# Loading the first six tiles as two halves of 64 partitions on two DMA queues

## The chip, the cores and the metric

The kernel runs on one core of a Trainium2 chip. The metric is the device time of one execution in microseconds (us); lower is better.

## The reference

A channel gate. The input is 384 x 384 pixels of 384 channels in bf16, 113 MB. The mean of each channel goes through a one-tap filter and a sigmoid, and scales that channel everywhere.

```python
g = jnp.einsum("bhwc->bc", x) / (H * W)
s = sigmoid(g * w1d[0])
return x * s[:, None, None, :]
```

## The kernel before

All of x is read once and all of the output is written once. 147,456 pixels are 1152 rows on each of 128 partitions; they are cut into 26 tiles of 45 or 44 rows (8 of 45, 18 of 44). The on-chip ring has room for six tiles.

Loads are issued by SP (SyncE), stores by ACT (ScalarE). Each of the two has its own DMA queue (q1 and q10 on the page of the kernel before, 3744 and 3746 packets). The profile counts 16 DMA engines, and in the packet records about 16 rows are in flight at a time, whether they come from one queue or from two; so the same 16 engines are taken to serve both. In the profile's lines PE is TensorE and DVE is VectorE. TensorE adds up every tile with a matrix of ones. After three tiles a provisional sigmoid `s_early` is taken from the rows seen so far, and VectorE multiplies tiles by it and ACT stores them. At the end the true sigmoid is compared with `s_early` bit for bit; only if they differ would a second pass run (in no run shown here did it). So the time is one pass over the data.

```python
TILE = 45
AHEAD_TILES = 3
...
plan.dma("scalar", w_one[0:1, 0:1], w1d.unsqueeze(0), writes=["w_one"])   # weight first
... # warm up the sigmoid's table; matmul and scaling of the weight

def load(place, n, r0):
    plan.dma("sync", at(place, n), dram(x_rows, r0, n), writes=rows(place, n))
...
for k, n in enumerate(sizes):
    place = ring.take(n)
    while inside and any(p < place + n and place < p + m for p, m, _ in inside):
        put(*inside.pop(0))          # multiply by s_early (vector), store (scalar queue)
    load(place, n, r0)
    inside.append((place, n, r0))
    add_rows(...)                    # n matmuls with ones
    if k == AHEAD_TILES - 1:
        ... # total <- acc (vector); s_early <- sigmoid(total) (scalar)
```

`plan` writes one instruction stream per engine in program order and puts semaphore waits where data need them. A load of a 45-row tile writes 34,560 bytes to each of 128 partitions, and in the trace it is 128 packets of that size. Below, "a row" of a load means such a packet of one partition.

Of the kernel before, what the change touches and what calls it, by code (L numbers as in the profile page):

```python
# [3 lines left out]
P = 128  # L4
# [5 lines left out]
ACT_F = mybir.ActivationFunctionType  # L10
# [113 lines left out]
TILE = 45  # L124
# [3 lines left out]
def bass_standalone__channel_attn_eca__vision_kernel(  # L128
# [7 lines left out]
    n_rows = B * H * W // P  # L136
    x_rows, o_rows = x.flatten_outer_dims(), out.flatten_outer_dims()

    def dram(view, r0, n):
        return view[r0 * P : (r0 + n) * P, :].rearrange("(p t) c -> p (t c)", p=P)  # L140

    ones = nc.alloc_sbuf_tensor("ones", [P, P], BF16)
    s_early = nc.alloc_sbuf_tensor("s_early", [P, C], BF16)
    s_true = nc.alloc_sbuf_tensor("s_true", [P, C], BF16)
    w_one = nc.alloc_sbuf_tensor("w_one", [1, 16], BF16)
    w_scaled = nc.alloc_sbuf_tensor("w_scaled", [P, 2], F32)
    warm = nc.alloc_sbuf_tensor("warm", [P, 2], F32)
# [3 lines left out]
    n_arena = nc.sbuf_bytes_remaining // (2 * C)  # L151
    arena = nc.alloc_sbuf_tensor("arena", [P, n_arena * C], BF16)
    acc = [nc.alloc_psum_tensor(f"acc{i}", [P, 512], F32) for i in range(3)]

    def at(r0, n):
        assert r0 + n <= n_arena
        return arena[:, r0 * C : (r0 + n) * C]

    def rows(r0, n):
        return [("sb", r) for r in range(r0, r0 + n)]  # L160

    def gate(place, n, s):
        s_b = s[:].unsqueeze(1).broadcast_to([P, n, C])
# [4 lines left out]
    early_rows = sum(sizes[:AHEAD_TILES])  # L168
    plan = Planner(nc, "a", 50)


    plan.op("gpsimd", lambda e: e.memset(warm[:, 0:1], 0.0), writes=["warm"])  # L172
    plan.op("vector", lambda e: e.memset(ones[:], 1.0), writes=["ones"])  # L173
    plan.dma("scalar", w_one[0:1, 0:1], w1d.unsqueeze(0), writes=["w_one"])
    plan.op(
        "scalar",
        lambda e: e.activation(warm[:, 1:2], warm[:, 0:1], ACT_F.Sigmoid),  # L177
        reads=["warm"],
        writes=["warm1"],
    )  # L180
    plan.op(
        "tensor",
        lambda e: e.matmul(  # L183
            acc[2][:, 0:1], ones[0:1, :], w_one[0:1, 0:1], start=True, stop=True
        ),
        reads=["ones", "w_one"],
        writes=["acc2"],
    )
    for i, n in enumerate((early_rows, n_rows)):
        plan.op(  # L190
            "vector",
            lambda e, i=i, n=n: e.tensor_scalar_mul(  # L192
                w_scaled[:, i : i + 1], acc[2][:, 0:1], 1.0 / float(P * n)
            ),
            reads=["acc2"],
            writes=[f"w_scaled{i}"],
        )

    def load(place, n, r0):
        plan.dma("sync", at(place, n), dram(x_rows, r0, n), writes=rows(place, n))  # L200

    def add_rows(place, n, bank, first, last):
        for i in range(n):
            plan.op(
                "tensor",
                lambda e, i=i: e.matmul(  # L206
                    acc[bank][:, :C],
                    ones[:],
                    at(place + i, 1),
                    start=first and i == 0,  # L210
                    stop=last and i == n - 1,
                ),
                reads=["ones"] + (rows(place, n) if i in (0, n - 1) else []),
                writes=[f"acc{bank}"],
                signal=i == n - 1,
            )

    def put(place, n, r0):
        plan.op(
            "vector",  # L220
            gate(place, n, s_early),
            reads=["s_early"] + rows(place, n),
            writes=rows(place, n),
        )
        plan.final.append(
            plan.dma("scalar", dram(o_rows, r0, n), at(place, n), reads=rows(place, n))
        )


    ring = Ring(n_arena)  # L230
    inside = []
    r0 = 0
    for k, n in enumerate(sizes):
        place = ring.take(n)
        while inside and any(
            p < place + n and place < p + m for p, m, _ in inside
        ):
            put(*inside.pop(0))
        load(place, n, r0)
        inside.append((place, n, r0))  # L240
        if k < AHEAD_TILES:
            add_rows(place, n, 0, k == 0, k == AHEAD_TILES - 1)
        else:
            add_rows(place, n, 1, k == AHEAD_TILES, k == len(sizes) - 1)
        r0 += n
        if k == AHEAD_TILES - 1:
            plan.op(
                "vector",
                lambda e: e.tensor_copy(total[:], acc[0][:, :C]),  # L249
                reads=["acc0"],  # L250
                writes=["total"],
            )
            plan.op(
                "scalar",
                lambda e: e.activation(  # L255
                    s_early[:], total[:], ACT_F.Sigmoid, scale=w_scaled[:, 0:1]
                ),
                reads=["total", "w_scaled0", "warm1"],
                writes=["s_early"],
            )  # L260
    for tile in inside:
# [6 lines left out]
        reads=["total", "acc1"],  # L268
        writes=["total"],
# [6 lines left out]
        reads=["total", "w_scaled1"],  # L276
        writes=["s_true"],
# [6 lines left out]
        reads=["s_true", "s_early"],  # L284
        writes=["total"],
# [4 lines left out]
        reads=["total"],  # L290
        writes=["wrong"],
# [4 lines left out]
        reads=["wrong"],  # L296
        writes=["redo"],
# [6 lines left out]
    r0 = 0  # L304
    for n in sizes:
        place = ring.take(n)
# [4 lines left out]
            reads=rows(place, n),  # L311
            writes=rows(place, n),
# [72 lines left out]
```

## Time and profile before

533.75 us is the median of the three runs given with the kernel (533.66 to 533.89).

| what | before | where it is read |
|---|---|---|
| span of the profiled run | 532.4 us | page, first line |
| DMA busy | nine tenths or more in all slices but the last | page, part 2 |
| mean rate, bytes moved | 426 GB/s, 226.66 MB | page, DMA lines |
| busiest compute engine | PE, 46% | page, part 1 |
| one row of 34,560 bytes on its DMA engine | 1.28 us | packet records of the trace |
| tile 2 landed; `s_early` made | 35.4 us; 45.8 us | chain of waits |

The page of the kernel before, its DMA lines: each digit or number is one of 40 equal slices of the span, 13.3 us long; DMA is the busy share of the 16 DMA engines in tenths.

```profile
span 532.4 us, 2500 instructions
...
DMA  9999999999999999999999999999999999999995
GB/s 371 418 450 421 411 415 454 418 449 417 447 416 449 414 448 425 434 442 423 432 444 424 432 443 421 434 444 415 439 444 421 434 440 424 434 442 423 432 440 241
DMA packets 7501, 226.66 MB, mean 426 GB/s; under 512 B 834, under 2 KB 834, under 8 KB 834
```

The DMA engines are the limit from the first slice to the last. In the first three slices there are only loads, later loads and stores, and the rate is the same: 16 engines x 34,560 B / 1.28 us = 432 GB/s. At that rate 226.5 MB of data take 524 us, so of a 532 us span at most about 8 us could be won.

The chain of waits of the kernel before, its start (start us, duration us, what):

```profile
1.63 33.79 DMA arena<-in_x_dram
...
35.46 9.09 PE acc L206 x45
...
45.16 0.62 ACT s_early L255
```

Nothing on this chain leaves the DMA idle: while TensorE adds tile 2 and the sigmoid is made, tiles 3 to 5 are still coming in (33 to 47 us: DMA share 1.01, 434 GB/s). That is why a chain through PE and ACT costs nothing here.

The stretch 2 to 42 us of the kernel before (start:end, length, busy us and count of instructions of PE, PE's weight loads, DVE, ACT and POOL, then TensorE's granted clock, DMA share and GB/s):

```profile
2.00:42.00 40.00, 23.84 (x122) 13.01 (x123) 0.22 (x2) 0.77 (x2) 0.00 (x0) 0.96 0.97 419
```

### The profile page before, as it was taken

To read this page: it belongs to the slowest core of one execution; us is meant where nothing else is said; L and a number is where in the kernel's file an instruction comes from. 1 tells how busy PE (TensorE), PEld (TensorE's weight loads), DVE (VectorE), ACT (ScalarE), POOL (GpSimd) and SP (SyncE) were. 2 spreads that over 40 slices of the span, in tenths; PEclk is the share of its full clock that TensorE was granted. 3 is DMA by queue.
4 is the path that set the end of the run, shared out by engine and by line. 5 is a ranking of instruction groups with operands and counts; after the bars stand their busy time and mean duration, and the time that the engine had idled before them with its cause. 6 is when DMAs were issued, how large, how long until landed. Compare 5 with 4: busy or idle time off the path is not lost.

```text
span 532.4 us, 2500 instructions
## 1 busy us (share of the span) xinstructions
PE 243.2 (46%) x1153; PEld 127.8 (24%) x1153; DVE 236.7 (44%) x34; ACT 2.7 (1%) x4; POOL 0.3 (0%) x5
## 2 busy tenths in 40 slices
PE   0979643347156156266266156266265255165100
PEld 0435311123023033133133033033132133032000
DVE  0006999551642642633633642632633642633700
ACT  1000000000000000000000000000000000000000
POOL 0000000000000000000000000000000000000000
PEclk9989867587686786775676686786675686786755
DMA  9999999999999999999999999999999999999995
GB/s 371 418 450 421 411 415 454 418 449 417 447 416 449 414 448 425 434 442 423 432 444 424 432 443 421 434 444 415 439 444 421 434 440 424 434 442 423 432 440 241
DMA packets 7501, 226.66 MB, mean 426 GB/s; under 512 B 834, under 2 KB 834, under 8 KB 834
## 3 DMA queue, kind: packets, MB, share of 16 engines
q1 hardware_dynamic: 3744, 113.25, 49.6%
q10 hardware_dynamic: 3746, 113.25, 49.3%
q8 instruction: 9, 0.15, 0.1%
q14 instruction: 2, 0.02, 0.0%
HBM read 113.25 MB, written 113.25 MB: 425 GB/s over the span
## 4 chain that ended last, share of the span: by engine, by line
another core or an unknown queue 63%; DMA 20%; DVE 7%; PE 3%; SPq 1%; issue 1%; ACT 0%; DVEq 0%
DMA arena<-in_x_dram 12%; DMA out_dram<-arena 8%; DVE arena L165 7%; PE acc L206 3%; SPq L91 1%; ACT s_early L255 0%; ACT s_true L273 0%; DVE total L281 0%; DVE total L249 0%; DVE wrong L289 0%; DVE total L267 0%; SPq L99 0%; DVE redo L295 0%; DVEq L99 0%
## 5 line engine op out<-in xcount | busy, mean ns | idle before, releaser
L206 PE MATMUL acc<-arena,ones 128*128 128x384 bf16 x1152 | 243.0, 383 | 249.2 <-DMA arena<-in_x_dram 249.2
L165 DVE TENSOR_TENSOR arena<-arena,s_early 128x16896 bf16<-128x16896 bf16 (+1 forms) x26 | 234.1, 9019 | 224.3 <-PE acc L206 223.6
L206 PEld LDWEIGHTS acc<-arena,ones 128*128 128x128 bf16 x1152 | 127.7, 113 | 364.2 <-DMA arena<-in_x_dram 258.9
L249 DVE COPY total<-acc 128x384 f32<-128x384 f32 x1 | 0.6, 558 | 42.1 <-PE acc L206 42.1
L273 ACT ACTIVATE s_true<-total,w_scaled 128x384 bf16<-128x384 f32 x1 | 0.6, 615 | 458.2 <-DVE total L267 458.2
L177 ACT ACT_TABLE_LOAD x1 | 1.3, 1283 | 1.3 <-PEq L370 1.3
L183 PE MATMUL acc<-w_one,ones 1*128 1x1 bf16 x1 | 0.2, 158 | 2.0 <-DMA w_one<-in_w1d_dram 2.0
L281 DVE TENSOR_TENSOR total<-s_true,s_early 128x384 f32<-128x384 uint16 x1 | 0.6, 559 | 0.7 <-ACT s_true L273 0.7
L255 ACT ACTIVATE s_early<-total,w_scaled 128x384 bf16<-128x384 f32 x1 | 0.6, 616 | 42.4 <-DVE total L249 42.4
L192 DVE TENSOR_SCALAR w_scaled<-acc 128x1 f32<-128x1 f32 x2 | 0.2, 153 | 1.2 <-PE acc L183 1.2
L183 PEld LDWEIGHTS acc<-w_one,ones 1*128 1x128 bf16 x1 | 0.1, 99 | 2.0 <-issue 2.0
L289 DVE TENSOR_REDUCE wrong<-total 128x1 f32<-128x384 f32 x1 | 0.6, 553 | 0.0
L267 DVE TENSOR_TENSOR total<-total,acc 128x384 f32<-128x384 f32 x1 | 0.5, 546 | 0.0
L173 DVE MEMSET ones<- 128x128 bf16 x1 | 0.2, 165 | 0.8 <-PEq L370 0.8
L177 ACT ACTIVATE warm<-warm 128x1 f32<-128x1 f32 x1 | 0.2, 203 | 0.0
L295 DVE CAST redo<-wrong 128x1 int32<-128x1 f32 x1 | 0.2, 154 | 0.0
L370 POOL MEMSET const-bfloat16-1.0<- 128x1 bf16 x1 | 0.1, 102 | 0.0
L370 POOL MEMSET const-uint8-127<- 128x1 uint8 x1 | 0.1, 102 | 0.0
L172 POOL MEMSET warm<- 128x1 f32 x1 | 0.1, 99 | 0.3 <-POOLq L370 0.3
L370 POOL MEMSET const-float32-0.0<- 128x1 f32 x1 | 0.1, 99 | 0.2 <-issue 0.2
L370 POOL MEMSET const-float32-1.0<- 128x1 f32 x1 | 0.1, 99 | 0.0
## 6 DMA issues: line engine op xcount, KB each, us to landing
arena<-in_x_dram SPq DMA_DIRECT2D x18, 4224.0 KB, 28.9
out_dram<-arena ACTq DMA_DIRECT2D x18, 4224.0 KB, 72.2
arena<-in_x_dram SPq DMA_DIRECT2D x8, 4320.0 KB, 31.0
out_dram<-arena ACTq DMA_DIRECT2D x8, 4320.0 KB, 58.7
w_one<-in_w1d_dram ACTq DMA_DIRECT2D x1, 0.0 KB
```

The source lines that it names most:

```text
L91: ("op", lambda e: e.dma_start(out, in_), self.pool[i], 16)
L165: return lambda e: e.tensor_tensor(v, v, s_b, ALU.mult)
L177: lambda e: e.activation(warm[:, 1:2], warm[:, 0:1], ACT_F.Sigmoid),
L183: lambda e: e.matmul(acc[2][:, 0:1], ones[0:1, :], w_one[0:1, 0:1], start=True, stop=True),
L206: lambda e, i=i: e.matmul(acc[bank][:, :C], ones[:], at(place + i, 1), start=first and i == 0, stop=last and i == n - 1,),
L249: lambda e: e.tensor_copy(total[:], acc[0][:, :C]),
L255: lambda e: e.activation(s_early[:], total[:], ACT_F.Sigmoid, scale=w_scaled[:, 0:1]),
L267: lambda e: e.tensor_tensor(total[:], total[:], acc[1][:, :C], ALU.add),
L273: lambda e: e.activation(s_true[:], total[:], ACT_F.Sigmoid, scale=w_scaled[:, 1:2]),
L281: lambda e: e.tensor_tensor(total[:], s_true[:].bitcast(U16), s_early[:].bitcast(U16), ALU.not_equal),
L289: lambda e: e.reduce_max(wrong[:], total[:], axis=mybir.AxisListType.X),
L370: nc = _bacc.Bacc("TRN2", target_bir_lowering=False, num_devices=1)
```

## The change

The intent is to use both DMA queues at the start, when there are no stores yet. Each of the first six tiles comes in as two loads: partitions 0 to 63 on SP's queue, 64 to 127 on ACT's. The weight fetch, which was the first thing on ACT's queue, moves behind the first tile.

```diff
-    def load(place, n, r0):
-        plan.dma("sync", at(place, n), dram(x_rows, r0, n), writes=rows(place, n))
+    def load(place, n, r0, halved):
+        to, of = at(place, n), dram(x_rows, r0, n)
+        if halved:
+            for h, queue in enumerate(("sync", "scalar")):
+                part = slice(h * P // 2, (h + 1) * P // 2)
+                plan.dma(queue, to[part], of[part], writes=rows(place, n, [h]))
+        else:
+            plan.dma("sync", to, of, writes=rows(place, n))
...
-        load(place, n, r0)
+        load(place, n, r0, halved=k < n_arena // TILE)      # k < 6
...
+        if k == 0:
+            weight()                                        # was ahead of the loop
```

ACT's issues follow the order of its program. The order is now: half 0, weight, table load and warm-up, halves 1 and 2, `s_early`, halves 3 to 5, then the stores.

More of the change, by code (lines that the diff above doesn't have):

```diff
@@ L157, in at, with rows @@
         return arena[:, r0 * C : (r0 + n) * C]
-    def rows(r0, n):
-        return [("sb", r) for r in range(r0, r0 + n)]
+    def rows(r0, n, halves=(0, 1)):
+        return [(h, r) for h in halves for r in range(r0, r0 + n)]
     def gate(place, n, s):
@@ L173, in bass_standalone__channel_attn_eca__vision_kernel @@
     plan.op("vector", lambda e: e.memset(ones[:], 1.0), writes=["ones"])
-    plan.dma("scalar", w_one[0:1, 0:1], w1d.unsqueeze(0), writes=["w_one"])
-    plan.op(
-        "scalar",
-        lambda e: e.activation(warm[:, 1:2], warm[:, 0:1], ACT_F.Sigmoid),
-        reads=["warm"],
-        writes=["warm1"],
-    )
-    plan.op(
-        "tensor",
-        lambda e: e.matmul(
-            acc[2][:, 0:1], ones[0:1, :], w_one[0:1, 0:1], start=True, stop=True
-        ),
-        reads=["ones", "w_one"],
-        writes=["acc2"],
-    )
-    for i, n in enumerate((early_rows, n_rows)):
-        plan.op(
-            "vector",
-            lambda e, i=i, n=n: e.tensor_scalar_mul(
-                w_scaled[:, i : i + 1], acc[2][:, 0:1], 1.0 / float(P * n)
-            ),
-            reads=["acc2"],
-            writes=[f"w_scaled{i}"],
-        )
-    def load(place, n, r0):
-        plan.dma("sync", at(place, n), dram(x_rows, r0, n), writes=rows(place, n))
+    def load(place, n, r0, halved):
[6 more added lines that the diff above has]
+            plan.dma("sync", to, of, writes=rows(place, n))
     def add_rows(place, n, bank, first, last):
@@ L227, in put, with weight @@
         )
+    def weight():
+        plan.dma("scalar", w_one[0:1, 0:1], w1d.unsqueeze(0), writes=["w_one"])
+        plan.op(
+            "scalar",
+            lambda e: e.activation(warm[:, 1:2], warm[:, 0:1], ACT_F.Sigmoid),
+            reads=["warm"],
+            writes=["warm1"],
+        )
+        plan.op(
+            "tensor",
+            lambda e: e.matmul(
+                acc[2][:, 0:1], ones[0:1, :], w_one[0:1, 0:1], start=True, stop=True
+            ),
+            reads=["ones", "w_one"],
+            writes=["acc2"],
+        )
+        for i, n in enumerate((early_rows, n_rows)):
+            plan.op(
+                "vector",
+                lambda e, i=i, n=n: e.tensor_scalar_mul(
+                    w_scaled[:, i : i + 1], acc[2][:, 0:1], 1.0 / float(P * n)
+                ),
+                reads=["acc2"],
+                writes=[f"w_scaled{i}"],
+            )
     ring = Ring(n_arena)
```

## The prediction

> **What bounds the kernel.** The DMA engines. The page shows DMA at 9 tenths in all slices but the last, 426 GB/s mean, 226.5 MB moved; no compute engine is above 46%. In the trace's packet records every 34,560-byte row takes 1.28 us on its DMA engine, load or store, and all 16 engines are occupied: 16 x 34,560 B / 1.28 us = 432 GB/s, also in the first 40 us where only loads run. At that rate 226.5 MB take 524 us of the 532.4 us span, so at most 8 us (1.5%) could be won. Two queues cannot make the load stage faster: one already runs it at the engines' rate. The first load is issued at 0.73 us, its packets start at 1.7 us; tile 2 has landed at 35.4 us; 9.1 us of matmuls, copy and sigmoid give s_early at 45.8 us (chain of waits). None of it leaves the DMA idle: tiles 3 to 5 are queued.
>
> **What the change removes.** Moving the weight fetch saves nothing: w_scaled was ready at 2.5 us and is needed at 45 us. Six more DMA issues cost 0.3 to 0.5 us each on ACT, off the path.
>
> **What it adds.** (1) ACT runs in program order: its half loads of tiles 3 to 5 now stand behind the s_early activation (instruction order). So ACT's load queue is empty from about 33 us (24 rows per DMA engine x 1.28 us after the start) until about 47 us (45.8 us, an issue, about 1 us to the first packet). In these 13.5 us only SP's halves, partitions 0 to 63, can move. [...] The kernel is DMA bound to its end, so nothing gives it back: 533.75 + 13.5 = 547 us.
>
> **Worse case.** With both queues full, every DMA engine alternates between the halves. If all write the lower half at one moment and then the upper, this stage is slowed too: at worst 61 us for all six tiles, likelier 25 to 45 us. **Better case.** If a half runs at the full 432 GB/s, work is conserved and the time stays at about 533.5 us.
>
> **Predicted: 547 us, range 533 to 582 us; faster by over 2% 0.01, within 2% 0.25, slower by over 2% 0.74.** All of it lies in the first 75 us; the rest should keep its 20 us per tile.
>
> **What would show it.** GB/s in slices 3 and 4 (27 to 53 us) falling from about 420 to well under 350; half-tile packets of about 2.5 us instead of 1.28 us while SP's halves run alone [...]; ACT's last three half loads issued right after s_early, near 46 us; the first store landing after 78 us; tile 3's matmuls starting after 45.7 us. Slices 0 to 2 at half their GB/s, and s_early well after 46 us, mean the worse case. [...]
>
> **What would make it wrong.** [...] an earlier first packet from using two queues (under 1 us).

The forecast's sum came to 533.75 + 13.5 = 547 us. Its terms are two of about 6.7 us, one for the 13.5 us in which SP's halves run alone and one for ACT's halves alone at the end. Both took a half alone to be slow by a figure that no run had shown by then. The "61 us" of the worse case is an estimate: 48 half rows for each DMA engine (six tiles of 128 rows on 16 engines), each longer by the 1.28 us that a row takes in the trace; that rows take twice as long was assumed. That the engines alternate between the halves and all write one half at a time was not shown then either; the rows in flight of the changed kernel show it below (16/0, then 0/16).

## The result, and the profile after

The changed kernel takes 595.78 us (median, 595.54 to 596.33) against 533.82 us for the kernel before in the same rounds. The ratio is 1.116, with a 95% interval of 1.1143 to 1.1176. Here and below a ratio is the one for the same rounds; it is not quite the ratio of the medians. The change costs 62 us. The prediction had said 547 us, and 582 us at most.

The page of the changed kernel, the same lines (a slice is now 14.9 us):

```profile
span 594.5 us, 2517 instructions
...
DMA  8999999999999999999999999999999999999996
GB/s 195 214 223 223 198 210 223 195 299 435 442 426 433 435 439 423 432 437 436 437 433 430 423 437 434 429 437 434 434 433 437 434 434 426 427 434 431 434 435 280
DMA packets 7597, 226.66 MB, mean 381 GB/s; under 512 B 930, under 2 KB 930, under 8 KB 930
```

Read the two DMA lines together. The busy digits are nearly unchanged, so a reader who looks only at "DMA busy" sees a saturated machine in both kernels. The GB/s line tells them apart: the first eight slices, 119 us, run at about half rate, and from the tenth slice on the kernel runs at its old rate (423 to 442 GB/s in all slices but the last). The same bytes are moved; the engines are occupied and slow.

The chain of waits of the changed kernel, its start:

```profile
2.56 49.01 DMA arena<-in_x_dram
...
72.45 10.43 PE acc L186 x45
...
83.49 0.62 ACT s_early L264
```

Tile 2 is complete at 72.3 us (35.4 us before), and `s_early` is there at 84.1 us (45.8 us before). Its stretches, both queues full first, then SP's halves alone, then both again, then ACT's halves alone:

```profile
2.00:72.00 70.00, 18.33 (x91) 9.86 (x91) 0.23 (x2) 1.49 (x2) 0.00 (x0) 0.85 1.03 221
74.00:85.00 11.00, 8.86 (x41) 4.51 (x39) 1.42 (x2) 0.61 (x1) 0.00 (x0) 0.80 1.04 212
88.00:100.00 12.00, 0.00 (x0) 0.00 (x0) 12.00 (x2) 0.00 (x0) 0.00 (x0) 0.50 0.90 199
105.00:122.00 17.00, 12.28 (x63) 6.72 (x64) 10.36 (x2) 0.00 (x0) 0.00 (x0) 0.78 1.07 218
```

All four stretches are at half rate (199 to 221 GB/s), with DMA share 0.90 to 1.07. It makes no difference whether one queue or both are at work. In the packet records a half tile's row takes 2.5 us when it starts as a row of the other queue ends, and 2.7 us when two rows of one queue follow each other; no row that started between 20 and 40 us took under 2.5 us. The sum is simple: each of 16 DMA engines handles 48 rows for six tiles (768 in all), and 48 x (2.5 to 2.7 us, less 1.28 us) is 59 to 68 us. The measured loss is 62 us. The whole loss is in the length of the rows.

Counting in the packet records how many rows of SP's and of ACT's queue are in flight, every 0.5 us from 7 to 15 us, shows something the page cannot (SP/ACT):

```
15/1 6/10 0/16 0/16 0/16 1/15 10/6 16/0 16/0 16/0 15/1 7/10 0/16 0/16 0/16 1/15 8/8
```

All 16 rows in flight are for the lower half of the partitions, then all for the upper half, and so on. Read as one row on each of the 16 DMA engines, they are in step. (From 27.7 us on, one of them is often out of step; more on this below.)

### The profile page after: what moved, and what is told of

Its sections match the earlier page's. It is cut to its first block, busy times and chain, and to the rows that moved or that the text cites. A ratio compares the mean times of both kernels' runs of the same rounds, so it can differ in the third digit from the quotient of the medians.

```text
span 594.5 us, 2517 instructions
## 1 busy us (share of the span) xinstructions
PE 243.5 (41%) x1153; PEld 128.0 (22%) x1153; DVE 236.9 (40%) x34; ACT 2.7 (0%) x4; POOL 0.3 (0%) x5
## 4 chain that ended last, share of the span: by engine, by line
another core or an unknown queue 64%; DMA 21%; PE 5%; DVE 3%; SPq 1%; ACTq 0%; issue 0%; ACT 0%; DVEq 0%
DMA arena<-in_x_dram 13%; DMA out_dram<-arena 8%; PE acc L186 5%; DVE arena L165 3%; SPq L91 1%; ACTq L91 0%; ACT s_early L264 0%; ACT s_true L282 0%; DVE total L290 0%; DVE total L258 0%; DVE wrong L298 0%; DVE total L276 0%; SPq L99 0%; DVE redo L304 0%
```

## The experiments

Three theories were put against each other at first. *Partition theory*: which partitions a load writes decides its rate, and the rows for some sets of partitions slow each other down, those of 0 to 63 among them. *Half-transfer theory*: any load of 64 partitions is slow. *Queue theory*: two load queues that alternate on the same DMA engines, or the number and order of the loads, cost the time. In the expectations the name of the partition theory, and the hardware supposed behind it, are cut, since no run shows that hardware: where a sentence starts with a marked cut, it tells what this theory expects, unless the text below it says otherwise. Unless it says otherwise, an edit below is against the changed kernel. Lines that only extend the bookkeeping of dependences, or allocate the target of a tiny load, are left out of the diffs.

### 1. Which partitions are slow: probes of shapes (p1_shapes)

The kernel before, with twelve single loads ahead of it on one queue, each waiting for the one before:

```diff
+    probe(0, 128)          # partitions p0 to p1, 45 rows of data each
+    probe(0, 64)
+    probe(64, 128)
+    probe(32, 96)
+    probe(0, 32)
+    probe(0, 128, 2)       # every second partition
+    probe(0, 96)
+    probe(0, 64, up=2)     # the same places, every second row of the source
+    probe(32, 96, up=2)
+    probe(0, 16)
+    probe(0, 8)
+    probe(0, 128)
```

> The kernel before, with twelve loads of single tiles (45 rows a partition) put ahead of it on one queue, each waiting for the one before: partitions 0-127; 0-63; 64-127; 32-95; 0-31; every second partition; 0-95; 0-63 and 32-95 from every second row of the source; 0-15; 0-7; 0-127 again. [...] rows of 34,560 bytes take about 1.28 us for 0-127 and for 32-95, about 2.5 us for 0-63, 64-127 and 0-31, more than 2.5 us for 0-15. Half-transfer theory (any transfer of 64 partitions is slow, whichever they are): 32-95 takes about 2.5 us too. HBM theory (the source rows collide): the loads from every second source row differ from those of adjoining rows.

Each window of the probe's trace covers one load from first to last packet. In order: 0-127, 0-63, 64-127, 32-95, 0-31, every second; the last column is GB/s.

```profile
1.74:13.80 12.06, 0.16 (x1) 0.10 (x1) 0.22 (x2) 1.03 (x2) 0.00 (x0) 1.00 0.91 367
15.53:26.69 11.16, 0.00 (x0) 0.00 (x0) 0.00 (x0) 0.00 (x0) 0.00 (x0) 1.00 0.94 198
28.74:39.74 11.00, 0.00 (x0) 0.00 (x0) 0.00 (x0) 0.00 (x0) 0.00 (x0) 1.00 0.96 201
41.99:48.35 6.36, 0.00 (x0) 0.00 (x0) 0.00 (x0) 0.00 (x0) 0.00 (x0) 1.00 0.93 348
49.72:55.48 5.76, 0.00 (x0) 0.00 (x0) 0.00 (x0) 0.00 (x0) 0.00 (x0) 1.00 0.90 192
57.61:65.18 7.57, 0.00 (x0) 0.00 (x0) 0.00 (x0) 0.00 (x0) 0.00 (x0) 1.00 0.77 288
```

Lines two and four are the experiment. Both loads have 64 partitions, the same source rows, the same size and the same queue; 0-63 takes 11.2 us (median row 2.72 us) and 32-95 takes 6.4 us (median row 1.28 us). The half-transfer theory falls. So does an explanation by the source: with every second source row, 0-63 still has a median row of 2.72 us and 32-95 of 1.28 us. The 32 partitions 0-31 are as slow as the 64, and every second partition is fast (median row 1.28 us; its window is stretched by a slow start). The 96 partitions 0-95 had a median row of 2.56 us. The 16 partitions 0-15 had a median row of 3.9 us and the eight partitions 0-7 one of 3.8 us, slower still.

### 2. Halves by rows, both halves on one queue, another cut (e1_rows, e2_one_queue, e3_middle)

e1_rows keeps two queues, two loads for each tile and the order of issue, but each half has all 128 partitions:

```diff
-            for h, queue in enumerate(("sync", "scalar")):
-                part = slice(h * P // 2, (h + 1) * P // 2)
-                plan.dma(queue, to[part], of[part], writes=rows(place, n, [h]))
+            top = (n + 1) // 2
+            for r, m, queue in ((0, top, "sync"), (top, n - top, "scalar")):
+                plan.dma(queue, at(place + r, m), of[:, r * C : (r + m) * C],
+                         writes=rows(place + r, m))
```

> The changed kernel with the halves cut by rows: each half has all 128 partitions and 23 or 22 of the 45 rows, still one on each queue, ACT's last three still behind the sigmoid. [...] 128 partitions run at full rate, so about 533.8 us, like the kernel before. Queue theory (two load queues that alternate on the same DMA engines, or twice the DMAs, cost the 62 us): about 595 us.

Measured: 533.99 us, ratio 1.0004 (0.9988 to 1.0021). Two queues, twelve loads and ACT's late halves cost nothing, and gain nothing.

e2_one_queue keeps the halves of 64 partitions and takes the second queue away:

```diff
-            for h, queue in enumerate(("sync", "scalar")):
+            for h, queue in enumerate(("sync", "sync")):
```

> The changed kernel with both halves of 64 partitions on the SP queue. [...] each half runs at half rate with one queue too, so 590 to 597 us. Queue theory: without the alternation back to about 534 us.

Measured: 592.67 us, ratio 1.1106 (1.1077 to 1.1134), rows of 2.5 to 2.7 us. Together the two runs dispose of the queue theory: the loss needs the halves and not the second queue.

e3_middle cuts the partitions elsewhere:

```diff
-            for h, queue in enumerate(("sync", "scalar")):
-                part = slice(h * P // 2, (h + 1) * P // 2)
-                plan.dma(queue, to[part], of[part], writes=rows(place, n, [h]))
+            for h, p0, p1, queue in ((0, 32, 96, "sync"), (1, 0, 32, "scalar"),
+                                     (2, 96, 128, "scalar")):
+                plan.dma(queue, to[p0:p1], of[p0:p1], writes=rows(place, n, [h]))
```

> The changed kernel with another cut of the partitions: SP loads 32 to 95, ACT loads 0 to 31 and 96 to 127. [...] SP's rows take about 1.28 us, ACT's about 2.5 us, so about half of the 62 us is lost, 560 to 570 us. Half-transfer theory: all rows take about 2.5 us, about 595 us.

Measured: 567.24 us, ratio 1.0626 (1.0608 to 1.0643), about half of the loss. Its stretches: both queues, SP's 32-95 alone, mostly ACT's quarters alone:

```profile
10.00:60.00 50.00, 21.09 (x101) 11.11 (x102) 0.23 (x2) 0.00 (x0) 0.00 (x0) 0.87 0.98 276
60.00:70.00 10.00, 6.21 (x37) 3.49 (x35) 3.07 (x2) 0.61 (x1) 0.00 (x0) 0.98 1.11 434
72.00:98.00 26.00, 12.86 (x61) 6.88 (x62) 25.09 (x4) 0.00 (x0) 0.00 (x0) 0.63 1.00 213
```

A load of 64 partitions, alone but for the last microsecond (ACT's next rows start at 68.96 us), runs at 434 GB/s when the partitions are 32 to 95, and loads of 0-31 and 96-127 run at 213 GB/s.

### 3. One to sixteen rows at once on chosen partitions (p2_ports)

The kernel before with 17 groups of four small loads ahead of it; for a load of m partitions with one row each the trace has m rows in flight at once (up to 16), which is read here as one on each of m DMA engines:

```diff
+    group((S, 0, 1, 1))        # queue, first, end, step of the partitions
+    group((S, 64, 65, 1))
+    group((S, 0, 2, 1))
+    group((S, 0, 8, 4))
+    group((S, 0, 128, 64))
+    group((S, 0, 64, 32))
+    group((S, 0, 4, 1))
+    ...
```

> The kernel before, with 17 small groups of loads put ahead of it, each of four loads of the same partitions (one row of 34,560 bytes a partition), each group waiting for the one before. On one queue: partition 0; 64; 0-1; 0 and 4; 0 and 64; 0 and 32; 0-3; every fourth of 0-15, of 0-31, of 0-63; every eighth of 0-127; every fourth of 32-95; every second of 0-127. On two queues at once: 0-1 beside 64-65; the same with one tiny load ahead of it on one DMA engine, to put two engines out of step; 0 beside 64. Then 0-63. [...] 1.28 us a row for single partitions, 0 and 4, 0 and 64, every fourth of 0-15, 0-31 and 32-95; about 2.5 us for 0-1, 0 and 32, every fourth of 0-63, every eighth of 0-127; over 2.5 us for 0-3; 0-1 beside 64-65 about 2.5 us in step and 1.28 us out of step. If it is a property of large half transfers[...], the two-partition groups all take 1.28 us. If being out of step does not help even two engines, the out-of-step group takes 2.5 us too.

Median time of a row, from the packet records:

```
partitions            us a row
0                     1.28
64                    1.34
0 and 4               1.28
0 and 64              1.28
0 and 1               2.71
0 and 32              2.71
0, 1, 2, 3            5.09
0,4,8,12              1.28
0,4,...,28            1.28
0,4,...,60            2.71
0,8,...,120           2.71
32,36,...,92          1.43 (1.28 at best)
every second, 64      1.28
0-63                  2.72
```

The medians are near those expected (2.71 us for "about 2.5 us"; 1.34 us for partition 64 and 1.43 us for every fourth of 32-95 in place of 1.28 us). Partitions 0 and 32 slow each other (2.71 us) and 0 and 64 do not (1.28 us), though both are two partitions on two DMA engines. Partitions 0 to 3 take 5.09 us a row, 4 x 34,560 B / 5.09 us = 27 GB/s together, the same as partition 0 alone (34,560 B / 1.28 us = 27 GB/s): in these loads the four rows together went no faster than one alone. What the rows that slow each other share on the chip, no trace here shows.

The two-queue groups held a surprise. Partitions 0-1 on SP beside 64-65 on ACT started at 2.3 us a row and, without any help, went to 1.6 to 1.9 us by the eighth row of each engine, as the two engines drifted apart, so that part of the time one was at the lower and the other at the upper pair (rows in flight 1/1 between 2/0 and 0/2). The group with the tiny load did the same a little sooner (1.4 us at its end). So being out of step helped two engines here. Neither of the two values expected, 2.5 us in step and 1.28 us out of it, was met cleanly.

### 4. The parts of the change alone (e4_weight_first, e8_weight_only, e6_one_tile, e7_early_act)

e4_weight_first puts the weight back in front and leaves the halves:

```diff
-        if k == 0:
-            weight()
...
+    weight()
     ring = Ring(n_arena)
```

> The changed kernel with the weight fetch and the sigmoid's warm-up back in front of the loads. The weight part of the change costs nothing in all theories that blame the halves: 592 to 597 us. If the weight's place mattered, nearer to 534 us.

Measured: 596.31 us, ratio 1.1173 (1.1154 to 1.1192).

e8_weight_only is the kernel before with only `weight()` moved behind the first tile:

```diff
+        if k == 0:
+            weight()
         r0 += n
```

> The kernel before with only the weight part of the change: the weight fetch and the warm-up of the sigmoid behind the first tile, all loads whole. All theories: no difference, 533 to 534.5 us.

Measured: 533.60 us, ratio 0.9999 (0.9982 to 1.0015). The weight part is free both ways.

e6_one_tile halves only the first tile:

```diff
-        load(place, n, r0, halved=k < n_arena // TILE)
+        load(place, n, r0, halved=k < 1)
```

> The changed kernel with only the first tile in halves, the other 25 whole on SP. [...] each halved tile costs 4.42 MB at about 216 instead of 432 GB/s, 10.2 us, so 542 to 545 us (a sixth of the 62 us). If a loss beyond this came from ACT's late halves, which are gone here, less than a sixth in each tile: nearer to 538 us.

Measured: 543.02 us, ratio 1.0173 (1.0156 to 1.019), so 9.3 us for one tile: below the 2% line, but clear of the noise. Six times that is 56 us of the 62 us. In the changed kernel some stretches have one queue alone, where rows take 2.7 us and not 2.5 us: its half rows average 2.61 us against 2.53 us here. Over 48 rows for each engine that is, as an estimate, 4 of the 6 us that are left.

e7_early_act issues ACT's six halves at the start, ahead of `s_early`, so that its load queue cannot run empty:

```diff
+    load(0, sizes[0], 0, halved=True)
     for k, n in enumerate(sizes):
...
+        if k == 0:
+            weight()
+            for j in range(1, n_arena // TILE):
+                load(sum(sizes[:j]), sizes[j], sum(sizes[:j]), halved=True)
```

> The changed kernel with all six ACT halves issued at the start, ahead of the sigmoid, so that ACT's load queue does not run empty. [...] a half is as slow alone as beside the other, so nothing comes back: 592 to 597 us. The prediction's term for the empty queue (13.5 us) as a cost of its own: about 582 us.

Measured: 594.13 us, ratio 1.1125 (1.1106 to 1.1144). The empty queue, which the prediction had made the centre of its sum, is worth under 3 us here (595.78 less 594.13 us), because beside the other queue a half is nearly as slow as alone (rows of 2.5 and 2.7 us).

### 5. One line that repairs it (e9_even_odd)

```diff
-                part = slice(h * P // 2, (h + 1) * P // 2)
+                part = slice(h, P, 2)
```

> The changed kernel with one line different: SP's half is the even partitions, ACT's the odd ones, still 64 partitions and 2.2 MB each, still two queues, the same order of issue. [...] every second partition ran at 1.28 us a row in both earlier probes. [...] 533 to 536 us. If 64-partition halves on two queues were slow for any other reason: 560 us or more.

Measured: 534.41 us, ratio 1.002 (1.0003 to 1.0037). Same queues, sizes, number of loads and order as the changed kernel, and 61 us less. The stretch that the kernel before ran at 419 GB/s:

```profile
2.00:42.00 40.00, 20.61 (x116) 11.71 (x117) 0.22 (x2) 1.49 (x2) 0.00 (x0) 1.00 1.01 428
```

It gains nothing over the kernel before, and nor does e1_rows: at 419 GB/s the stage was near the 432 GB/s of rows of 1.28 us already.

### 6. Do the engines have to be in step? (e5_stagger, p3_steps)

If rows slow each other only while they are for the same half (rows for partitions 0 and 64 together took 1.28 us in p2_ports), the stage with both queues full need not be slow: some engines could write 0-63 while the others write 64-127. e5_stagger tries to force that. It is e4_weight_first with a tiny load of 8 partitions, meant to take up one turn of SP's queue on 8 of the 16 engines:

```diff
                 plan.dma(queue, to[part], of[part], writes=rows(place, n, [h]))
+                if r0 == 0 and h == 0:
+                    plan.dma("sync", odd[:, :], of[0:8, 0:16], writes=["odd"])
```

> As e4_weight_first, with one tiny load of 8 partitions x 32 bytes on SP behind SP's first half. It takes up one turn of SP on eight of the 16 DMA engines, so that these write one half while the other eight write the other. [...] rows take about 1.28 us while both queues have halves, 2.7 us only while SP's run alone, so about 547 us, the time predicted. If the slow rows do not depend on which half the other engines are at: about 595 us.

Measured: 596.26 us, ratio 1.1166 (1.1147 to 1.1185). The trick, read from the rows in flight, worked for part of the time: from 21 to 28 us half of the engines were at each half (rows in flight SP/ACT from 22 us: 8/8 9/7 10/6 8/8 8/8 8/8), from 28.5 to 37 us all were in step again, and from 38.5 to 48 us apart again. And yet no row between 20 and 48 us, in step or not, took under 2.4 us. This contradicted the theory in that simple form, so p3_steps tried it with loads of 2, 4, 8 and 16 partitions, one row for each, read again as one on each of as many engines; each size once plain and once with a tiny load on half of the engines:

```diff
+    for k, step in ((2, 1), (4, 16), (8, 8), (16, 4)):
+        group(k, step, False)     # six loads on SP (from partition 0), six on ACT (from 64)
+        group(k, step, True)      # the same, a tiny load on k/2 partitions behind SP's second
```

> The kernel before, with eight groups of loads ahead of it. In each, SP sends six loads to the lower and ACT six to the upper 64 partitions, one row per DMA engine, on 2, 4, 8 and 16 engines[...]; each size once plain and once with a tiny load on half of the engines behind SP's second load. In the last probe two engines[...] drifted apart and went from 2.3 to 1.6 us a row. If being out of step helps a pair whatever the other engines do, all sizes drift to well under 2.3 us or do so after the tiny load. If many engines[...] hold one another up, 2 and 4 engines get faster and 16 stay at about 2.5 us, as in the changed kernel and e5_stagger.

Median row at the start and at the end of each group:

```
engines   plain               with the tiny load
2         2.51 -> 2.37-2.70   2.37 -> 1.29
4         2.24 -> 1.29        2.31 -> 1.29
8         2.21 -> 2.07        2.15 -> 1.53
16        2.52 -> 2.52        2.41 -> 1.53
```

The windows of the 16-engine groups, plain and then shifted:

```profile
155.00:182.00 27.00, 0.00 (x0) 0.00 (x0) 0.00 (x0) 0.00 (x0) 0.00 (x0) 1.00 0.95 206
196.00:206.00 10.00, 0.00 (x0) 0.00 (x0) 0.00 (x0) 0.00 (x0) 0.00 (x0) 1.00 1.07 384
```

Sixteen engines stay in step for as long as the group lasts when left alone, and go from 206 to 384 GB/s when a tiny load is put on half of them. Small sets sometimes drift apart by themselves and sometimes do not (2 engines drifted in p2_ports and not here in the plain group).

### 7. The same in the whole kernel (e12_fours, e13_fours_stagger, e10_stagger4, e11_stagger_alt)

e12_fours is e4_weight_first with each half cut into four loads of every fourth partition, the form of the last probe; e13_fours_stagger adds one tiny load:

```diff
-            for h, queue in enumerate(("sync", "scalar")):
-                part = slice(h * P // 2, (h + 1) * P // 2)
-                plan.dma(queue, to[part], of[part], writes=rows(place, n, [h]))
+            for r in range(4):
+                for h, queue in enumerate(("sync", "scalar")):
+                    part = slice(64 * h + r, 64 * h + 64, 4)
+                    plan.dma(queue, to[part], of[part], writes=rows(place, n, [4 * h + r]))
+                    # e13 only:
+                    if r0 == 0 and r == 1 and h == 0:
+                        plan.dma("sync", odd[:, :], of[0:8, 0:16], writes=["odd"])
```

> As e4_weight_first, with each half of 64 partitions cut into four loads of every fourth partition (16 partitions, one row per DMA engine)[...]. [...] as slow as the changed kernel, 590 to 602 us, rows about 2.5 us.

> e12_fours with one tiny load of 8 partitions on SP among its first loads. In the last probe this put eight of 16 engines out of step and rows went from 2.5 to 1.5 us. If being in step is what made the stage with both queues full slow, rows fall to about 1.5 us there and stay at 2.5 to 2.7 us where one queue's halves run alone: 550 to 570 us. If not: as e12_fours.

Measured: e12_fours 589.70 us, ratio 1.1056 (1.1 to 1.1112), just below what was expected; e13_fours_stagger 574.03 us, ratio 1.0763 (1.0712 to 1.0813), 4 us above what was expected. The rows in flight from 24 us on, every 0.5 us, e12 first:

```
10/6 3/13 0/16 0/16 2/14 6/10 14/2 16/0 16/0 14/2 8/7 0/16 0/16 0/16 2/14 9/7 16/0
8/8 7/9 8/8 8/8 9/7 8/8 8/8 7/9 6/10 8/8 9/7 12/4 8/8 8/8 4/13 8/8 8/8
```

The stretch of e12_fours with both queues full:

```profile
20.00:40.00 20.00, 8.81 (x45) 4.74 (x45) 0.00 (x0) 0.00 (x0) 0.00 (x0) 0.96 0.98 221
```

The stretches of e13_fours_stagger: both queues full, SP alone, both full again after ACT's queue had run empty:

```profile
20.00:40.00 20.00, 15.38 (x74) 8.29 (x75) 0.00 (x0) 0.00 (x0) 0.00 (x0) 0.91 0.97 344
45.00:58.00 13.00, 9.71 (x45) 5.04 (x45) 0.56 (x1) 0.61 (x1) 0.00 (x0) 0.74 1.02 209
65.00:80.00 15.00, 0.00 (x0) 0.00 (x0) 15.00 (x3) 0.00 (x0) 0.00 (x0) 0.50 0.95 221
```

One load of 256 bytes takes the first stage from 221 to 344 GB/s; all else in the two kernels is the same. The last line says why not more came of it: after ACT's queue had been empty only four of the 16 engines were out of step (12/4, 4/12) and the rate was 221 GB/s. No row that started between 66 and 80 us took under 2.3 us, so four engines out of step sped up nobody, not even themselves.

e10_stagger4 and e11_stagger_alt ask why e5_stagger did nothing. They are e5_stagger with the tiny load on 4 partitions, and with 15 tiny loads of 1 to 15 partitions by turns on both queues, meant to shift the engines by different numbers of turns. In each expectation the first range is for the case that this helps, the last for the case that it does not:

```diff
-                    plan.dma("sync", odd[:, :], of[0:8, 0:16], writes=["odd"])
+                    plan.dma("sync", odd[0:4, :], of[0:4, 0:16], writes=["odd"])          # e10
...
+                    for k in range(1, 16):                                                # e11
+                        plan.dma(("sync", "scalar")[k % 2], odd[0:k, 16 * k : 16 * (k + 1)],
+                                 of[0:k, 0:16], writes=[("odd", k)])
```

> e5_stagger with the tiny load on 4 partitions instead of 8[...]. e5_stagger did not help; [...] rows under 2.3 us for part of the engines and a time some us below 596. If being out of step does not help these loads at all: 594 to 597 us.

> e5_stagger with 15 tiny loads of 1 to 15 partitions, by turns on SP and ACT[...]. [...] rows under 2 us while both queues have halves, 545 to 575 us. If not, or if being out of step does not help these loads: 594 to 598 us.

Measured: e10_stagger4 595.64 us (ratio 1.1168), no effect; e11_stagger_alt 588.78 us (ratio 1.1039), between the two ranges that were expected. In e11, 73 of the 237 rows that started between 30 and 60 us took under 1.5 us, which no row of e5 or e10 did. So some rows of whole halves can be sped up by tiny loads too: the 15 of e11 did it, the one of 8 partitions in e5 and the one of 4 in e10 did not. Why these, was not shown.

## Why the prediction was wrong

- **The bound: right.** DMA engines at their rate, 1.28 us a row, 432 GB/s with one queue. e1_rows (533.99 us) and e9_even_odd (534.41 us) show that two queues gain nothing.
- **The weight: right.** e8_weight_only and e4_weight_first show no effect. The weight itself came late, at 31.1 us (29.8 us after its issue) instead of 1.9 us, and nobody needed it before 83 us.
- **A half alone is slow: right.** The prediction could show no run for it. In p1_shapes 0-63 had a median row of 2.72 us and 198 GB/s, and in the changed kernel SP's halves alone ran at 212 GB/s. But it is not so for any 64 partitions: 32-95 had a median row of 1.28 us.
- **ACT's late halves: right as an event, wrong as the cost.** ACT's queue was empty between 72.3 us, when the last of its third half had landed, and 83.5 us, when the next was issued (the prediction had said 33 to 47 us). But e7_early_act, without that gap, is at 594.13 us.
- **The step that failed** is the sum behind the 13.5 us. It counts only the stretches of one half alone and so takes for granted that with both queues full the two halves together run at the full 432 GB/s. They ran at 221 GB/s. The text's "worse case" named what really happens, "If all write the lower half at one moment and then the upper", and its limit, "at worst 61 us for all six tiles", is the measured 62 us. But it was judged unlikely in its full size ("likelier 25 to 45 us"), and the prediction gives no number for that. So the path was wrong (the loss is in every half row, not in the gap on ACT's queue), and the term for it was mis-sized: the stage with both queues full lost half of its rate from 2 to 72 us, and so did the rest. p3_steps and e12 show 16 engines mostly in step when nothing shifts them (206 and 221 GB/s), and e13 shows that shifting them brings much of the rate back (344 GB/s). That being in step is what held this stage at half rate is shown for the loads of e12 and e13, where one tiny load makes the difference; for the changed kernel's own loads only e11 speaks, weakly, and e5 and e10 speak against its simplest form.
- **The signs named in advance** were of use: half-rate slices 0 to 2 and an `s_early` well after 46 us were put down as the mark of the worse case, and both came.

What stays open: how the rows of a load of 64 adjoining partitions are dealt to the 16 engines, and so which of the rows in flight slow each other in the changed kernel; and what on the chip they share. Two observations do not fit the simple picture, in which pairs of engines slow each other, and only while both write the same half. From 27.7 us on, in stretches, one engine of the changed kernel is out of step with the other 15 (rows in flight 1/15 and 15/1), and neither its rows nor any other became faster than 2.5 us, though the other 15 were at the other half. And in e13_fours_stagger four engines out of step (65 to 80 us) changed nothing. A rival is therefore not excluded: that more than pairs of engines hold each other up, so that few out of step gain nothing. The expectation of p3_steps named it, and its plain groups (4 engines drifted to 1.29 us, 8 to 2.07 us, 16 stayed at 2.52 us) agree with it.

## What to carry to other kernels

When a load is cut by partitions, try which partitions each piece has: here that decided its rate. 0-63, 64-127 and 0-31 ran at half rate (198, 201 and 192 GB/s in p1_shapes), 32-95 and every second partition at full rate (median rows of 1.28 us), and a cut along the rows kept all 128 (533.99 us). Two halves 0-63 and 64-127 on two queues did not add up to a whole (221 GB/s): nearly all engines worked on the same half at the same time, which was shown to be the cause only for halves cut into four loads (221 and 344 GB/s in e12 and e13). Read DMA busy and GB/s together: the slow stage looked fully busy (DMA share 1.03 at 221 GB/s), and only the bytes per microsecond, or the time of one packet, showed it. And before adding a queue, compare the packet time with the rate already reached; here one queue was at 432 GB/s and there was nothing to win.
